# Unmasked even-head queries, score matmuls over 16 rows, more reciprocals broadcast by DMA, and a reordered head and tail in a two-layer attention and feed-forward kernel

## The chip, the cores and the metric

The kernel runs on one NeuronCore of a Trainium2 chip. The core has TensorE (PE: matrix products), VectorE (DVE), ScalarE (ACT: the exponentials here), GpSimd (POOL) and SyncE (SP: it issues DMA transfers). The metric is device time in microseconds (us); a smaller number is better. A half per cent of it is about 8 us.

## The reference

The input x has 2048 rows of 512 numbers. Two layers are applied to it one after the other, and both use the same weights. Cut to what matters:

```python
def _A_ref(x, wqkv, wo):                       # 32 heads of 16 columns each
    q, k, v = split((x @ wqkv))
    scores = einsum("bhqd,bhkd->bhqk", q, k) * 16 ** -0.5
    return merge(einsum("bhqk,bhkd->bhqd", softmax(scores), v)) @ wo

def _B_ref(x, w1, w2):                         # 512 -> 1792 -> 512
    return maximum(x @ w1, 0) @ w2

for layer in range(2):
    x = x + _A_ref(_layernorm(x), wqkv, wo)
    x = x + _B_ref(_layernorm(x), w1, w2)
```

A layer's softmax has 32 x 2048 x 2048 scores, so 134 million exponentials. In units of 128 x 512 scores that is 2048 blocks a layer, 4096 in all.

## The kernel before, in words

**Layout.** Scores are kept transposed: 128 keys lie on the partitions, and 512 queries (256 in the last chunks of layer 1) on the columns. A tile of Q or K holds eight heads, four pairs of them; each pair lies on 32 partitions, 16 for the even head (e = 0) and 16 for the odd one (e = 1). A score matmul multiplies all 32 partitions of a pair, with Q masked so that only the wanted head counts: `q_masked` (L637) reads the Q projection out of PSUM once and writes it twice, multiplied by two columns of `qmask` that hold the softmax scale for one head and zero for the other. Four such matmuls, one for each pair, run in four strips of 32 rows of TensorE.

**Slots.** The main loop (`while units`) works in slots of three blocks of 512 score columns, in one of two PSUM tiles `ps_s`. ScalarE takes the exponential of the whole slot (L1323, 1536 columns), or of two blocks of it (1024 columns); then VectorE takes the third block, with an approximation of its own: a line (`lin`, L1008, integer arithmetic that yields the bits of a float), and, once two such halves make a pair, a `chain` of bit operations and products (`step`, `cube`, L1049 to L1064). The products of exponentials and V (L914) add up in one PSUM bank, `ps_o`, for each segment, which is one head (of each of four pairs) for one chunk of queries and some of the keys. V carries columns of ones, so the same matmuls give the softmax sums.

**The end of a segment** (`finish_segment`). VectorE copies `ps_o` to a tile `u` (L836), or adds stored partial sums to it (L834) when the segment is the second part of a head ("load"). SyncE gathers the row of sums to a small tile `c`, VectorE takes the reciprocals (L860), SyncE writes them back, and they are spread over the head's rows into `r`: by a DMA that GpSimd issues (L863), or, where the segment is "quick", by a shuffle on VectorE (L873). A product (L849) writes the attention output `ot`. A segment is quick if it has partial sums to load or is the last of its chunk. The last two segments take the reciprocals after the spread, without the small transfers (`direct`).

**The other work**, the projections, layer norms, output projection and feed-forward of each chunk, is cut into groups of matmuls (L442) with an evacuation by VectorE, and is fitted between the slots. The order is written when the program is built: a planner keeps clocks for TensorE, VectorE and ScalarE (`now_pe`, `now_dve`, `exp_end`) with costs and lags (`R_LAG` = 10500 ns until a broadcast by DMA is there, `C_LAG` = 3600 ns) and picks what comes next. `rank` orders VectorE's tasks: chains rank below other tasks, but above them when the current segment has at most `HASTE` blocks left. A score matmul is repeated where the planner sees TensorE idle (`times`), to keep it busy. At run time each engine executes its list in order and waits on semaphores.

**Layer norm.** `ln_stats` (L477, L478) takes statistics of a tile of 128 rows, `ln_rstd` and `ln_newton` the reciprocal root (a seed from bits and Newton steps; the steps on GpSimd in the main loop, on VectorE in the head and the tail), `ln_apply` (L519) the normalisation.

**Head and tail.** In the head the first four tiles of x are normalised, transposed and projected to K, Q and V for the first slots; dummy matmuls (L1082) run meanwhile. In the tail, after the last exponential, the last 256 rows go through the output projection, layer norm and feed-forward. The 14 column blocks of w1 come through four rotating buffers `w1buf`; `load_w1` (L675) issues the next load when a buffer has been used, in the tail as well.

## Time and profile before

| what | value |
|---|---|
| median of 3 runs | 1608.02 us (1604.52 to 1611.87) |
| profiled execution, its own time | 1608.03 us |
| profiled execution, span of its instructions | 1606.2 us |
| mean granted TensorE clock | 0.992 |
| ScalarE busy | 1558.0 us (97%) |
| VectorE busy | 1505.7 us (94%) |
| TensorE busy (matmul) | 1446.1 us (90%) |
| first exponential starts | 16.74 us |
| last exponential ends | about 1576.7 us |

The profile gives for each group of instructions its source line, engine, operation, what it writes and reads, and the count; after the bar the busy time, the mean duration of one in ns, and the idle time of the engine just before them, with the instructions that ended it. Instructions of one engine can overlap by a little, so the mean duration is somewhat more than the busy time divided by the count. In a view by stretches each engine has its busy time in the stretch; then come the granted clock of TensorE as a share of full speed, the share of time of the DMA engines, and GB/s.

### The profile page before, as it was taken

The numbers are of one execution on the slowest core, as the hardware profiler recorded it, in microseconds if no ns is written. First come the engines' busy times: TensorE is split into PE (matmuls) and PEld (weight loads), VectorE is DVE, ScalarE is ACT, GpSimd is POOL, SyncE is SP. The second block draws the span as 40 slices with busy tenths as digits, with TensorE's granted clock in tenths as the row PEclk, the third lists the DMA queues.
The fourth block names the chain that finished last, engine by engine and source line by source line (L and its number), as shares of the span: only waits on it lengthen the run. The fifth ranks groups of instructions, "written<-read, shape, count | busy, mean of one in ns | idle before, by whom it ended". The sixth has DMA issues, their size and how long they took to land. (4 is left out here: it accounts for less than half of the span.)

```text
span 1606.2 us, 45384 instructions
## 1 busy us (share of the span) xinstructions
PE 1446.1 (90%) x19833; PEld 541.9 (34%) x19833; DVE 1505.7 (94%) x3012; ACT 1558.0 (97%) x1385; POOL 92.9 (6%) x279
## 2 busy tenths in 40 slices
PE   7988888999999988999889998889989999998997
PEld 3322222322332332232223333223334444544454
DVE  7779999999999999999899999899999999999994
ACT  6999999999999999999999999999999999999994
POOL 2000001000010010100100000001001010010100
PEclk9999999999999999999999999999999999999999
DMA  5000000210001100120001000000210211212031
GB/s 164 2 2 2 2 2 9 47 29 10 9 17 40 28 16 2 27 50 10 15 2 27 21 2 1 2 4 9 54 24 17 42 30 29 59 28 54 14 62 47
DMA packets 113928, 40.61 MB, mean 25 GB/s; under 512 B 103328, under 2 KB 111264, under 8 KB 113728
## 3 DMA queue, kind: packets, MB, share of 16 engines
q1 hardware_dynamic: 101696, 26.21, 7.2%
q0 software_dynamic: 10688, 10.18, 3.6%
q8 instruction: 155, 2.54, 0.7%
q10 hardware_dynamic: 1344, 1.31, 0.2%
q14 instruction: 45, 0.37, 0.1%
HBM read 24.38 MB, written 2.10 MB: 16 GB/s over the span
## 5 line engine op out<-in xcount | busy, mean ns | idle before, releaser
L1323 ACT ACTIVATE e<-ps_s 128x1536 bf16<-128x1536 f32 (+1 forms) x1366 | 1548.1, 1364 | 12.4 <-PE ps_s L1314 7.7
L1314 PE MATMUL ps_s<-q,ktp 32*128 32x512 bf16 (+1 forms) x6192 | 613.6, 341 | 112.2 <-ACT e L1323 97.5
L914 PE MATMUL ps_o<-e,vaug 128*32 128x512 bf16 (+1 forms) x4262 | 501.0, 346 | 16.6 <-DVE u L836 6.8
L1008 DVE TENSOR_SCALAR lin<-ps_s 128x512 int16<-128x512 f32 x680 | 462.3, 684 | 32.9 <-PE ps_s L1314 27.4
L1314 PEld LDWEIGHTS <-ktp 32*128 32x128 bf16 x6192 | 199.9, 91 | 561.5 <-issue 417.5
L914 PEld LDWEIGHTS <-vaug 128*32 128x32 bf16 x6032 | 171.5, 94 | 305.0 <-issue 286.2
L1049 DVE TENSOR_SCALAR step<-lin 128x1024 int16<-128x1024 int16 x680 | 266.2, 417 | 1.1 <-PE ps_o L914 0.4
L1060 DVE TENSOR_TENSOR cube<-step 128x1024 f16<-128x1024 bf16 x340 | 230.2, 680 | 0.9
L1064 DVE TENSOR_TENSOR cube<-cube,lin 128x1024 bf16<-128x1024 f16 x340 | 229.5, 677 | 0.0
L914 PE MATMUL ps_o<-step,vaug 128*32 128x512 bf16 (+1 forms) x858 | 154.3, 341 | 0.0
L442 PE MATMUL ps_f<-xnT,w 128*32 128x512 bf16 (+1 forms) x2016 | 147.4, 345 | 5.7 <-DVE ht L695 3.7
L442 PE MATMUL ps_f<-w,ht 128*32 128x512 bf16 x1624 | 147.1, 381 | 1.6 <-DVE q L637 0.6
L914 PE MATMUL ps_o<-cube,vthird 128*32 128x512 bf16 (+1 forms) x804 | 140.0, 339 | 0.0
L914 PE MATMUL ps_o<-lin,vaug 128*32 128x512 bf16 (+1 forms) x858 | 118.9, 341 | 4.6 <-DVE u L836 3.7
L442 PE MATMUL ps_f<-xnT,wqkv 128*32 128x512 bf16 (+1 forms) x1312 | 106.7, 363 | 3.6 <-DVE vaug L623 1.8
L863 POOL DMA_DIRECT2D r<-u x52 | 36.9, 710 | 1170.2 <-DVE step L1049 383.3
L442 PE MATMUL ps_f<-wo,ot 128*32 128x512 bf16 x960 | 87.1, 381 | 1.5 <-DVE x L661 0.7
L695 DVE TENSOR_SCALAR ht<-ps_f 128x512 bf16<-128x512 f32 x105 | 71.8, 684 | 3.6 <-PE ps_f L442 3.0
L442 PEld LDWEIGHTS <-w 128*32 128x32 bf16 x2016 | 58.4, 96 | 36.0 <-issue 19.2
L637 DVE TENSOR_TENSOR q<-ps_f,masks 128x1024 bf16<-128x1024 f32 (+1 forms) x51 | 53.5, 1049 | 3.5 <-PE ps_s L1314 2.6
L442 PEld LDWEIGHTS <-ht 128*32 128x32 bf16 x1624 | 47.0, 96 | 27.3 <-issue 12.1
L849 DVE SCALAR_TENSOR_TENSOR ot<-u,masks,r 128x512 bf16<-128x512 f32 (+2 forms) x82 | 51.0, 624 | 1.1
(86 smaller groups left out, 653.4 us busy)
## 6 DMA issues: line engine op xcount, KB each, us to landing
w<-in_B_w_dram SPq DMA_DIRECT2D x140, 128.0 KB
r<-u POOLq DMA_DIRECT2D x25, 256.0 KB, 7.3
r<-u POOLq DMA_DIRECT2D x27, 128.0 KB, 4.9
out_dram<-x SPq DMA_DIRECT2D x16, 128.0 KB
x<-in_A_x_dram SPq DMA_DIRECT2D x14, 128.0 KB
w<-in_B_w_dram SPq DMA_DIRECT2D x1, 1792.0 KB
wqkv<-in_A_wqkv_dram ACTq DMA_DIRECT2D x2, 512.0 KB
c<-u SPq DMA_DIRECT2D x48, 8.0 KB
```

The costliest lines, as they stand in the source:

```text
L442: nc.tensor.matmul(out[cols], lhsT[:, cols], rhs, start=i % k == 0, stop=i % k == k - 1, tile_position=(0, 32 * g), skip_group_check=True,)
L637: return nc.vector.tensor_mul(out=qbuf[n % 2][:, :, 0:w], in0=b.rearrange("p (e q) -> p e q", e=1).to_broadcast((P, 2, w)), in1=qmask.rear ...
L695: nc.vector.tensor_scalar(out=out, in0=sums, scalar1=0.0, scalar2=None, op0=ALU.max)
L849: nc.vector.scalar_tensor_tensor(out=ot[t][:, at_column + a : at_column + a + w], in0=u[:, a : a + w], scalar=mask[e], in1=r[:, a : a + w] ...
L863: nc.gpsimd.dma_start(out=r[:, 0:width], in_=bass.AP(tensor=sums.tensor, offset=sums.offset, ap=[list(sums.ap[0]), [0, 32], [1, width]],),)
L914: nc.tensor.matmul(ps_o[32 * g : 32 * g + 32, 0 : sg["w"]], values[:, 4 * sg["T"] + g, 2 * e : 2 * e + 32], rhs, start=g not in sg["begun" ...
L1008: first = nc.vector.tensor_scalar(out=lin[which][:, half * QS : (half + 1) * QS], in0=src, scalar1=EXP_BIAS, scalar2=0.0, op0=ALU.add, op1 ...
L1049: nc.vector.tensor_scalar(out=stair, in0=line, scalar1=keep, scalar2=put, op0=ALU.bitwise_and, op1=ALU.bitwise_or,)
L1060: (609, lambda: nc.vector.tensor_mul(out=power, in0=mantissa, in1=mantissa)),
L1064: (609, lambda: nc.vector.tensor_mul(out=power.bitcast(BF16), in0=power, in1=line.bitcast(BF16))),
L1314: nc.tensor.matmul(b[:, a : a + sg["w"]], kt[32 * g : 32 * g + 32, kc : kc + P], qbuf[sg["n"] % 2][32 * g : 32 * g + 32, sg["e"], 0 : sg[" ...
L1323: ex = nc.scalar.activation(out=eb[:, 0 : place[m]], in_=b[:, 0 : place[m]], func=ACTF.Exp, scale=1.0 / (LOG2E * UNIT),)
```

## The change

- **Q and scores.** The Q projection is copied with the scale as a factor, unmasked, for the even heads (`q_raw`), and a second instruction masks that copy for the odd heads (`q_odd`). A score matmul of an even head works over the first 16 partitions of its pair, one of an odd head over all 32. `qmask` is gone.
- **Reciprocals.** A segment with partial sums to load is quick only if it is among the last three of its chunk; the others are spread by DMA. Spread and product are tasks of their own.
- **Chains.** The raised rank now holds for the chains of every segment with at most 8 blocks left, counting all blocks and not only VectorE's, instead of the current segment with at most 12.
- **V.** A slot no longer forces the V of its keys to be made; the products with V are taken only when their V is there.
- **Layer norm.** The statistics of a chunk are taken first and aggregated together (`ln_seed`); the seed takes one bit operation less; in the head and the tail the root (`ln_root`) has one third-order step and one Newton step in place of three Newton steps.
- **Head.** Only the first V tile is made ahead of the loop, its copy goes to VectorE, the copies of the transposed x change engines, and there are more dummy matmuls.
- **Tail.** The last segment's sums are read out of PSUM with no copy. w1 for the last chunk is loaded when the last but two chunk ends: four blocks in `w1buf`, ten in tiles that held K of layer 0.

```diff
-    HASTE = 12
+    HASTE = 8
...
-        return 1.5 if sg is segs[seg_at[0]] and sg["left"] <= HASTE else 3
+        return 1.5 if sg["left"] <= HASTE else 3
...
-        st = stats[i % 2]
-        nc.vector.bn_stats(out=st[:], in_=x_t[tt][:])
-        nc.vector.bn_aggr(out=mv[ln_n(tag)][:, i, :], in_=st[:])
+        nc.vector.bn_stats(out=stats[ln_n(tag)][:, i, :], in_=x_t[tt][:])
...
+    def ln_root(tag, rows):
...
+        ln_seed(tag, rows, GAIN)
+        a, y, t1 = va_[n][:, 0:rows], ya_[n][:, 0:rows], ta_[n][:, 0:rows]
+        stt = nc.vector.scalar_tensor_tensor
+        nc.vector.tensor_mul(out=t1, in0=y, in1=y)
+        nc.vector.tensor_mul(out=t1, in0=t1, in1=a)
+        stt(out=t1, in0=t1, scalar=-10.0 / 3.0, in1=t1, op0=ALU.add, op1=ALU.mult)
+        stt(out=y, in0=t1, scalar=5.0, in1=y, op0=ALU.add, op1=ALU.mult)
+        stt(out=t1, in0=y, scalar=-0.5 / GAIN, in1=y, op0=ALU.mult, op1=ALU.mult)
+        nc.vector.tensor_mul(out=t1, in0=t1, in1=a)
+        stt(out=y, in0=t1, scalar=1.5, in1=y, op0=ALU.add, op1=ALU.mult)
...
-    def q_masked(n, b, w=QS):
-        return nc.vector.tensor_mul(
-            out=qbuf[n % 2][:, :, 0:w],
-            in0=b.rearrange("p (e q) -> p e q", e=1).to_broadcast((P, 2, w)),
-            in1=qmask.rearrange("p (e q) -> p e q", q=1).to_broadcast((P, 2, w)),
+    def q_raw(n, b, w=QS):
+        return nc.vector.tensor_scalar(
+            out=qbuf[n % 2][:, 0, 0:w], in0=b, scalar1=SCALE * LOG2E * UNIT, scalar2=None,
+            op0=ALU.mult,
+        )
+
+    def q_odd(n, w=QS):
+        nc.vector.tensor_scalar(
+            out=qbuf[n % 2][:, 1, 0:w], in0=qbuf[n % 2][:, 0, 0:w], scalar1=mask[1],
+            scalar2=None, op0=ALU.mult,
         )
...
         def fin(b):
-            q_masked(n, b, w)
-            mark(("q", n))
+            q_raw(n, b, w)
+            evac.appendleft((76 + 0.26 * w, 0.0, odd))
...
-        if n < len(chunks) * NF:
+        if n < len(chunks) * NF - NF + NW1:
...
+        if (l, j) == (1, LAST - 2):
+            for ft in range(NF):
+                home = (
+                    w1buf[((l * NQS + LAST) * NF + ft) % NW1] if ft < NW1
+                    else (kt01 + kt2)[(ft - NW1) // 2][:, ft % 2, :].rearrange(
+                        "p (c f) -> p c f", c=NDC
+                    )
+                )
+                w1_last.append(home)
+                if ft >= NW1:
+                    nc.sync.dma_start(
...
-        quick = sg["load"] is not None or ended[l, j] == NT
+        quick = ended[l, j] == NT or sg["load"] is not None and ended[l, j] >= NT - 2
...
+            source = ps_o if last else u
...
-    idle_matmuls(18)
+    idle_matmuls(24)
...
-        copy = nc.scalar.copy if i % 2 else nc.vector.tensor_copy
+        copy = nc.vector.tensor_copy if i > 1 else nc.scalar.copy
...
-    for kb in range(2):
-        b = plain(v_mms(kb))
-        uses(nc.scalar.copy(out=v_out(0, kb), in_=v_in(b)), in_bank[0])
-        mark(("v", 0, kb))
-    work.extend(v_group(0, kb) for kb in range(2, TPC))
+    b = plain(v_mms(0))
+    uses(nc.vector.tensor_copy(out=v_out(0, 0), in_=v_in(b)), in_bank[0])
+    mark(("v", 0, 0))
+    work.extend(v_group(0, kb) for kb in range(1, TPC))
...
-    now_pe[0] = 12000.0
-    now_dve[0] = 13400.0
-    exp_end = {-1: 13600.0, 0: 13600.0}
+    now_pe[0] = 13160.0
+    now_dve[0] = 14500.0
+    exp_end = {-1: 12600.0, 0: 13600.0}
...
-        for sg, kb, g in taken:
+        for sg, kb, g in now:
             sg["left"] -= 1
...
+                rows = slice(32 * g, 32 * g + 16 * (1 + sg["e"]))
...
-                    kt[32 * g : 32 * g + 32, kc : kc + P],
-                    qbuf[sg["n"] % 2][32 * g : 32 * g + 32, sg["e"], 0 : sg["w"]],
+                    kt[rows, kc : kc + P],
+                    qbuf[sg["n"] % 2][rows, sg["e"], 0 : sg["w"]],
...
-        for sg, kb, g in now:
-            run_until(("v", sg["l"], kb))
```

## The prediction
> **What bounds the kernel now.** I read the page's first two parts, then the groups of instructions kept apart by shape, the waits of ScalarE, and the stretches and timelines of head, tail and worst place. The page:

> ```profile
> span 1606.2 us, 45384 instructions
> PE 1446.1 (90%) x19833; PEld 541.9 (34%) x19833; DVE 1505.7 (94%) x3012; ACT 1558.0 (97%) x1385; POOL 92.9 (6%) x279
> ACT  6999999999999999999999999999999999999994
> ```

> ScalarE is full from the second slice to the last but one. The groups by shape (busy us, mean ns of one, idle before):

> ```profile
> L1323 ACT ACTIVATE e<-ps_s 128x1536 bf16<-128x1536 f32 x685 | 1026.9, 1574 | 8.2 <-PE ps_s L1314 4.2 <-PE ps_o L914 3.6
> L1323 ACT ACTIVATE e<-ps_s 128x1024 bf16<-128x1024 f32 x680 | 733.1, 1153 | 4.2 <-PE ps_s L1314 3.5 <-PE ps_o L914 0.4
> L637 DVE TENSOR_TENSOR q<-ps_f,masks 128x1024 bf16<-128x1024 f32 x35 | 42.6, 1217 | 2.4 <-PE ps_s L1314 1.7 <-PE ps_f L442 0.4
> L873 DVE STREAM_SHUFFLE r<-u 128x512 f32<-128x512 f32 x23 | 16.7, 727 | 0.0
> ```

> So the time is a head until the first exponential, one stream of 1366 exponentials with only 12.4 us of visible idle time, and a tail. A block of 512 scores that VectorE takes over is worth 1574 - 1153 = 421 ns of ScalarE. The head and the tail, from ScalarE's timeline (start, duration):

> ```profile
> 14.79 0.59 ACT L1128 CAST vaug<-ps_f 128x512 bf16<-128x512 f32 x1 [1.14 <-PE ps_f L1116]
> 15.65 0.59 ACT L1128 CAST vaug<-ps_s 128x512 bf16<-128x512 f32 x1 [0.28 <-PE ps_s L1116]
> 16.74 1.45 ACT L1323 ACTIVATE e<-ps_s 128x1536 bf16<-128x1536 f32 x1 [0.51 <-PE ps_s L1314]
> ...
> 1566.61 10.10 ACT L1323 ACTIVATE e<-ps_s 128x1536 bf16<-128x1536 f32 x8
> 1581.14 1.07 ACT L1387 CAST x<-ps_s 128x512 bf16<-128x512 f32 x2 [4.42 <-PE ps_s L1377]
> ```

> Head 16.7, stream to 1576.7, tail 29.5 us. Where the stream's idle time lies, by stretches (length, busy of PE, PEld, DVE, ACT, POOL, then the granted clock):

> ```profile
> 152.00:154.00 2.00, 0.92 (x11) 0.35 (x14) 2.00 (x4) 1.60 (x3) 0.00 (x0) 1.00 0.00 0
> 154.00:156.00 2.00, 1.22 (x15) 0.31 (x13) 1.09 (x3) 0.86 (x1) 0.00 (x0) 0.61 0.03 8
> 158.00:160.00 2.00, 2.00 (x15) 0.24 (x9) 1.14 (x2) 1.02 (x1) 0.00 (x0) 0.50 0.00 0
> ...
> 1588.00:1590.00 2.00, 2.00 (x10) 1.05 (x8) 0.42 (x1) 0.38 (x1) 0.00 (x0) 0.51 0.19 43
> ```

> VectorE is full (2.00 of 2.00) while TensorE has nothing to do (0.92), then the clock halves and ScalarE starves for ten microseconds: in 152 to 166 it is busy 9.22 of 14, 4.8 lost. The same pattern at 268 to 276 loses 1.0 and at 390 to 402 1.2. These three dips hold 7.0 of the 12.4 us. The last row is such a dip in the tail.

> [...] the longest idle stretch ahead of the tail's dip is 1.77 us (1584.58 to 1586.35), so partial idleness suffices. [...] 16 rows instead of 32 should cost a score matmul nothing. No 16-row matmul is in this trace. [...] the split q is one slow pass of 512 and a cheap second one. The trace agrees: 684 ns for 128x512 out of PSUM, 404 for the bf16 normalisation and 293 for the 544-wide vthird.

> **The change, part by part**, against the profiled execution: span 1606.2, its own time 1608.03 us, 1.8 around it, which is the median of the runs (1608.02).

> *Head, 2.2 us.* Measured before: last stats instruction done 6.7, normalisation 9.14, first K matmul 12.00, q 13.92 to 15.15, scores 16.31, exponential 16.74. The root takes 12 small instructions from 6.76 to 9.14, 0.20 each; 9 remain: 0.6 earlier; the four aggregations after the four stats run back to back, about 0.05. Copies of xnT: ScalarE takes the first two, VectorE the last two (0.42 instead of 0.59 for the last), another 0.15. First K matmul about 11.2. The K and Q weights don't block: x loads that wait for the same semaphores are issued by SyncE at 9.54 and 9.92; the one behind V's weights at 12.74. K and q take 1.89 (eight matmuls), to 13.1; the raw copy 0.68, to 13.8; the odd half and V's copy come after it, and the even heads don't need them. V's four matmuls end about 14.0, three score matmuls follow at once, without the 12 of the next q group (0.83) that stand ahead of them now, nor ScalarE's two V casts. Exponential at about 14.4 to 14.6: 2.2 saved. If V's weights came late, 0.5 less. Six more dummy matmuls (0.21 each warm) end near 8, before the transposes.

> *Stream, 3.4 us.* The built program has 677 wide and 688 narrow exponentials where there were 685 and 680: 8 x 0.421 = 3.4. VectorE pays with four chains: two line steps (1.37), two step passes (0.83), two products (1.36), 3.56 each, +14.2. It gets back: 36 wide q at 1.22 become 0.684 + 0.40 (0.29 at the least), -4.8 (to -8.8); 16 narrow ones 0.683 become 0.42 + 0.25, nothing; 11 shuffles of 0.727 gone, -8; one small instruction of 0.17 less in 15 roots, -2.6; one V copy more in the stream and one in the head, +1.4. Net about zero: VectorE stays at 94%. The matmuls rise by 92 of 19833 (all fillers among the scores), nothing while ScalarE is busier.

> *The dips, 3 us, my least certain term.* At 150.9 to 153 VectorE ran a shuffle (0.72), a product (0.75) and, just before, a 1.23 us q; a line step came late and score matmuls waited 1.25 us for it: then the clock fell. The shuffles of such segments become DMAs and the q stays in one piece of 0.68, so this place should lose less, and the raised rank of chains that are soon needed brings their results earlier. Bounds: 7.0 if all three dips vanish, -7 if as much comes anew elsewhere. I take 3: somewhat more than half of the largest dip.

> *More broadcasts on POOL's queue, nothing.* 36 wide ones instead of 25. They land 4.6 to 7.8 us after issue; with about 2.5 from reciprocal to issue that is at most 10.3, under the 10.5 that the planner waits, and no VectorE wait on such a landing is in the list of waits. What waits behind one on POOL is a root of twelve small instructions, planned with 5 us. Uncovered, each late microsecond stops VectorE's queue, a line step with it.

> *w1 loaded ahead.* The 10 SyncE issues of 128 KB move from the tail to the end of the last but two chunk. They stand before one 4 KB column read: 10 x 0.37 to 0.95 us of issue, hidden if the segment's sums come later than that. In the tail SyncE's loads now take 1588.40 to 1597.9, and the feed-forward matmuls at 1599.00 wait: steps of 0.87 (1596.73, 1597.60) become 1.40, 0.53 saved.

> *Tail, 1.25 + 0.7.* Dropping the copy of the last sums (0.47) is worth nothing: TensorE's 17 matmuls from 1577.26 end at the same time as the last product (1580.89), and the first cast at 1581.14 waits for TensorE. The root: 3 x 0.20 plus 0.06 of stats = 0.7. The w1 wait: 0.53. The idle stretch shrinks from 1.77 to about 1.1, so the dip at 1588.4 (some 2.9 us at half clock, 1.4 lost) may go: even odds, 0.7.

> Sum: 2.2 + 3.4 + 3.0 + 1.25 + 0.7 = 10.5; 1608.0 - 10.5 = 1597.5.

> **Rivals.** *A, only the ends pay.* New dips eat what the stream gains: 2.2 + 1.25 = 3.5, 1604.5. For it: the planner's order changes everywhere, waits on TensorE are scattered (18 for scores); against: VectorE's heaviest spot is relieved. *B, all dips go:* 2.2 + 3.4 + 7.0 + 1.25 + 1.4 = 15.3, 1592.8. For it: the three have one cause; against: the two later ones have no shuffle. *C, slower: broadcasts come late.* Short segments end every 6 to 8 us between 1030 and 1075, where shuffles are now replaced; if two overlapping 256 KB broadcasts land later than the planner's 10.5 us, VectorE's queue stands, TensorE idles and the clock halves. To end above 1616 it must lose 8.1 plus the 10.5 expected, 18.6 us, 1.7 for each of 11: landings some 9.5 us after issue (10.5 - 2.5 + 1.7), where 7.8 was the longest. *D, the edit doesn't act:* 16 rows are no faster, and are not counted as faster; if they cost even 10 ns each on half of 6285 matmuls, run four abreast, 8 us of a TensorE with 10% free, about 1 on the end.

> **How the numbers follow.** The sum as worked 0.50 (own range 1592 to 1603), A 0.27, B 0.15, C 0.08 (D inside the first). Half a per cent, about what a measurement tells from no change, is below 1600.0 or above 1616. Below: 0.72 of the first, all of B, a tenth of A, 0.54. Above: C, 0.08. The range 1589 to 1611 leaves out C and the far side of B.

> **What would show it.** First exponential at 14.5, narrow ones 688, no clock of 0.5 near 150 to 166, tail of 27.5 to 28.3 from the last exponential, no wait on w1 in it. Wrong if ScalarE's idle time in the stream is over 12 us, or VectorE waits for broadcasts.

## The result, and the profile after

The changed kernel took 1667.99 us (median of 4 runs, 1661.17 to 1673.46), the kernel before 1607.34 beside it: a ratio of 1.037, 95% interval 1.032 to 1.042. It became some 60 us slower where some 10 us faster was forecast. The profiled execution has a span of 1671.5 us. Its page, the lines that answer to those shown of before, with the row of the granted clock:

```profile
span 1671.5 us, 45644 instructions
PE 1538.1 (92%) x19925; PEld 542.6 (32%) x19925; DVE 1497.3 (90%) x3043; ACT 1567.2 (94%) x1383; POOL 102.7 (6%) x290
ACT  7999889999999999999999999979899999899994
PEclk9988668999999999899988998858899999999899
```

ScalarE does the same work as before and is 94% busy instead of 97%. TensorE is busy for 92 us more, with 0.5% more matmuls: it ran slower. The last row shows where. The granted clock falls to 0.5 or 0.6 in two regions, near 160 to 250 us and near 1100 us, where the ScalarE row has two of its 8s and its 7. The groups by shape:

```profile
L1367 ACT ACTIVATE e<-ps_s 128x1536 bf16<-128x1536 f32 x677 | 1010.8, 1549 | 40.0 <-PE ps_s L1358 36.6 <-PE ps_o L948 1.6
L1367 ACT ACTIVATE e<-ps_s 128x1024 bf16<-128x1024 f32 x688 | 735.1, 1131 | 31.2 <-PE ps_s L1358 29.5
L1358 PE MATMUL ps_s<-q,ktp 16*128 16x512 bf16 x1939 | 342.6, 424 | 39.0 <-ACT e L1367 33.7 <-DVE ktp L588 1.2 <-DVE u L860 0.6
L1358 PE MATMUL ps_s<-q,ktp 32*128 32x512 bf16 x1960 | 338.8, 413 | 33.2 <-ACT e L1367 29.6 <-DVE lin L1055 0.4 <-DVE mv L482 0.2
```

The exponentials are the 677 wide and 688 narrow ones that the prediction counted, and each takes no longer than before. But ScalarE stands idle for 71.2 us before them instead of 12.4, and nearly all of that is ended by score matmuls. The last two rows are a trap. The mean duration of a 16-row score matmul (424 ns) is hardly above that of a 32-row one (413), so nothing seems to be wrong with 16 rows. A view by stretches shows that both kinds suffer in the same places (length, busy time of PE, PEld, DVE, ACT, POOL, then the granted clock):

```profile
156.00:186.00 30.00, 29.94 (x194) 5.53 (x196) 22.29 (x43) 23.65 (x20) 0.68 (x1) 0.50 0.07 12
186.00:200.00 14.00, 11.92 (x128) 3.60 (x123) 12.64 (x25) 13.49 (x14) 0.68 (x1) 0.98 0.12 21
200.00:230.00 30.00, 29.75 (x197) 5.74 (x199) 22.20 (x43) 23.30 (x21) 0.00 (x0) 0.50 0.02 2
...
280.00:360.00 80.00, 72.55 (x860) 23.84 (x856) 79.06 (x160) 80.00 (x72) 6.07 (x15) 1.00 0.18 37
```

For 30 us at a time TensorE is busy without a gap (29.94 of 30) at a clock of 0.50, and ScalarE gets work for 23.65 of the 30. Between 280 and 360, where projections and feed-forward matmuls are fitted between the scores, nothing is lost. In the first region the clock falls (at 155.9, 200.2 and 244.6 us) some microseconds after score matmuls of even heads begin to prevail, near 152, 196 and 240, and returns twice (at 186.6 and 231.0) some ten microseconds after those of odd heads have taken over, and once (at 261.7) when projections come in.

### The profile page after: what moved, and what is told of

The parts are those of the page before. It is cut to its first block, busy times and chain, and to the rows that moved or that the text cites. A ratio compares the mean times of both kernels' runs of the same rounds, so it can differ in the third digit from the quotient of the medians.

```text
span 1671.5 us, 45644 instructions
## 1 busy us (share of the span) xinstructions
PE 1538.1 (92%) x19925; PEld 542.6 (32%) x19925; DVE 1497.3 (90%) x3043; ACT 1567.2 (94%) x1383; POOL 102.7 (6%) x290
## 4 chain that ended last, share of the span: by engine, by line
ACT 60%; PE 23%; DVE 13%; issue 2%; DMA 1%; SPq 1%; ACTq 0%; DVEq 0%
ACT e L1367 60%; PE ps_s L1358 9%; PE ps_o L948 7%; PE ps_f L442 4%; DVE lin L1055 4%; DVE step L1096 2%; DVE cube L1111 2%; DVE cube L1107 2%; PE ps_s L1419 1%; DVE ht L705 1%; SPq L770 1%; DMA c<-u 1%; DVE q L638 0%; DVE ot L878 0%; DMA wqkv<-in_A_wqkv_dram 0%
## 5 line engine op out<-in xcount | busy, mean ns | idle before, releaser
L1367 ACT ACTIVATE e<-ps_s 128x1536 bf16<-128x1536 f32 (+1 forms) x1366 | 1558.5, 1338 | 71.2 <-PE ps_s L1358 66.1
L1358 PE MATMUL ps_s<-q,ktp 32*128 32x512 bf16 (+3 forms) x6245 | 660.3, 365 | 91.4 <-ACT e L1367 80.3
L948 PE MATMUL ps_o<-e,vaug 128*32 128x512 bf16 (+1 forms) x4252 | 526.7, 365 | 11.4 <-DVE u L862 4.4
L1358 PEld LDWEIGHTS <-ktp 32*128 32x128 bf16 (+1 forms) x6245 | 196.4, 93 | 583.6 <-issue 436.5
L948 PE MATMUL ps_o<-step,vaug 128*32 128x512 bf16 (+1 forms) x868 | 166.7, 362 | 3.0 <-DVE step L1096 3.0
L442 PE MATMUL ps_f<-xnT,w 128*32 128x512 bf16 (+1 forms) x2016 | 152.9, 355 | 5.0 <-DVE ht L705 3.4
L442 PE MATMUL ps_f<-w,ht 128*32 128x512 bf16 x1624 | 147.4, 381 | 2.1 <-DVE ht L705 1.3
L948 PE MATMUL ps_o<-cube,vthird 128*32 128x512 bf16 (+1 forms) x814 | 146.8, 358 | 0.2 <-DVE cube L1111 0.2
L948 PE MATMUL ps_o<-lin,vaug 128*32 128x512 bf16 (+1 forms) x868 | 129.6, 365 | 3.7 <-DVE u L862 2.4
L892 POOL DMA_DIRECT2D r<-u x63 | 45.2, 717 | 1219.3 <-DMA u<-c 378.9
L442 PE MATMUL ps_f<-xnT,wqkv 128*32 128x512 bf16 (+1 forms) x1312 | 107.6, 374 | 3.8 <-DVE vaug L624 0.9
L442 PE MATMUL ps_f<-wo,ot 128*32 128x512 bf16 x960 | 92.3, 401 | 1.0 <-DVE x L671 0.4
L442 PEld LDWEIGHTS <-w 128*32 128x32 bf16 x2016 | 60.0, 98 | 35.4 <-issue 19.9
L442 PEld LDWEIGHTS <-ht 128*32 128x32 bf16 x1624 | 45.9, 96 | 27.7 <-issue 12.5
L948 PEld LDWEIGHTS <-vthird 128*32 128x32 bf16 x814 | 41.3, 97 | 33.1 <-issue 29.5
L878 DVE SCALAR_TENSOR_TENSOR ot<-u,masks,r 128x512 bf16<-128x512 f32 (+1 forms) x78 | 49.4, 633 | 0.3 <-DMA r<-u 0.3
```

The costliest lines, as they stand in the source:

```text
L442: nc.tensor.matmul(out[cols], lhsT[:, cols], rhs, start=i % k == 0, stop=i % k == k - 1, tile_position=(0, 32 * g), skip_group_check=True,)
L878: nc.vector.scalar_tensor_tensor(out=ot[t][:, at_column + a : at_column + a + w], in0=u[:, a : a + w], scalar=mask[e], in1=r[:, a : a + w] ...
L892: nc.gpsimd.dma_start(out=r[:, 0:width], in_=bass.AP(tensor=sums.tensor, offset=sums.offset, ap=[list(sums.ap[0]), [0, 32], [1, width]],),)
L948: nc.tensor.matmul(ps_o[32 * g : 32 * g + 32, 0 : sg["w"]], values[:, 4 * sg["T"] + g, 2 * e : 2 * e + 32], rhs, start=g not in sg["begun" ...
L1358: nc.tensor.matmul(b[:, a : a + sg["w"]], kt[rows, kc : kc + P], qbuf[sg["n"] % 2][rows, sg["e"], 0 : sg["w"]], start=True, stop=True, til ...
L1367: ex = nc.scalar.activation(out=eb[:, 0 : place[m]], in_=b[:, 0 : place[m]], func=ACTF.Exp, scale=1.0 / (LOG2E * UNIT),)
```

## The experiments

**Two theories.** R: 16 active rows count as less activity for TensorE's clock, so the clock halves. P: the planner's new order leaves TensorE idle, so the clock halves as it did in the three dips of before. Four kernels tell them apart. The line numbers differ by a few between them. Each ratio is to the kernel before as it ran beside that experiment (median 1608.95 us for these four, of which the one with masked Q stands further down, 1605.77 us for the later ones), and a clock is the mean of an execution.

**The change with 32 rows.** All of the change, but the even heads' score matmuls over 32 rows again. Q stays unmasked there, so the even heads' scores mix both heads of a pair: the masking is left out.

```diff
-                rows = slice(32 * g, 32 * g + 16 * (1 + sg["e"]))
+                rows = slice(32 * g, 32 * g + 32)
```

> The changed kernel with one edit: the score matmuls of the even heads work over 32 rows again, with the unmasked Q. The even heads' scores then hold both heads of a pair, so this kernel leaves the masking of the even heads out; order, instructions and durations are otherwise those of the changed kernel. Theory R (16 active rows count as less activity for TensorE's clock, so it halves in stretches that have little else to do): the mean clock goes back to 0.985 or more and the time to about 1600 us (1594 to 1608), what the rest of the change is worth. Rival P (the planner's new order, with V taken late, other chain ranks and more broadcasts, leaves TensorE idle and so lets the clock fall): the clock stays at 0.92 to 0.94 and the time at 1660 to 1673 us.

1604.39 us, ratio to before 0.997 (0.9958 to 0.9983), clock 0.986 to 0.996 instead of 0.924 to 0.935. The instructions and their order are those of the changed kernel, and 63.6 us are gone. The same two stretches:

```profile
156.00:186.00 30.00, 25.11 (x274) 7.48 (x271) 29.03 (x57) 30.00 (x28) 1.35 (x2) 1.00 0.11 18
200.00:230.00 30.00, 25.32 (x282) 7.67 (x283) 29.49 (x60) 30.00 (x29) 0.00 (x0) 1.00 0.02 2
```

TensorE has more gaps here (25.11 of 30 busy) than in the changed kernel, and keeps its full clock. P falls as the cause of this loss.

**The kernel before with 16 rows.** Q stays masked, and only the rows of the even heads' scores change.

```diff
+                rows = slice(32 * g, 32 * g + 16 * (1 + sg["e"]))
...
-                    kt[32 * g : 32 * g + 32, kc : kc + P],
-                    qbuf[sg["n"] % 2][32 * g : 32 * g + 32, sg["e"], 0 : sg["w"]],
+                    kt[rows, kc : kc + P],
+                    qbuf[sg["n"] % 2][rows, sg["e"], 0 : sg["w"]],
```

> The kernel before with one edit: the score matmuls of the even heads work over the first 16 rows of their pair; Q stays masked, so the values are the same. Theory R: the clock falls to 0.92 to 0.94, and the time rises to 1650 to 1680 us, with the half-clock stretches where even heads run without feed-forward work. Rival P: 1607 us within half a per cent, clock 0.99.

1660.23 us, ratio 1.033 (1.028 to 1.038), clock 0.934 to 0.948, so a little above the forecast in part. This edit alone makes 51.3 us of the loss (1608.95 to 1660.23), and its interval overlaps that of the whole change. The 16 rows that it takes away held zeros in Q, so rows that only multiplied zeros counted too. Its exponentials as one group, in an execution of 1649.86 us:

```profile
L1324 ACT ACTIVATE e<-ps_s 128x1536 bf16<-128x1536 f32 (+1 forms) x1366 | 1556.8, 1343 | 44.3 <-PE ps_s L1315 37.0 <-PE ps_o L914 4.9
```

**The change with 32 rows in the repeats.** Where the planner repeats score matmuls to keep TensorE busy, all but the last pass go over 32 rows. Only the last pass's scores are read.

```diff
-        for _ in range(times):
+        for rep in range(times):
...
-                rows = slice(32 * g, 32 * g + 16 * (1 + sg["e"]))
+                rows = slice(32 * g, 32 * g + (16 * (1 + sg["e"]) if rep == times - 1 else 32))
```

> The changed kernel with one edit: where a score matmul is repeated to keep TensorE busy, the repeats before the last one work over 32 rows for the even heads too; the last one, which writes what is used, over 16. Theory R: part of the activity comes back, so the clock lies between 0.94 and 0.985 and the time between 1610 and 1655 us. Rival P: no change from the changed kernel, 1660 to 1673 us.

1635.48 us, ratio 1.016 (1.010 to 1.022), clock 0.951 to 0.973. It gives back about half of the loss (1667.99 with 16 rows in the repeats, 1604.39 with 32 everywhere): more rows in matmuls whose results are thrown away made this kernel faster.

**The kernel before with 24 rows** for the even heads (the slice above with 24 in place of 16).

> The kernel before, with the score matmuls of the even heads over 24 rows instead of 32 (16 gave 1660.2 us, 32 gave 1608.9, its own time). Theory R: the fewer active rows, the oftener the clock falls: between the two, about 1615 to 1640, clock 0.96 to 0.985. If it is not the number of rows but the form (any matmul that doesn't fill its row group is handled otherwise), 24 rows cost what 16 do, about 1660.

1626.31 us, ratio 1.012 (1.009 to 1.015), clock 0.969 to 0.978. So 32, 24 and 16 rows make 1606 to 1609, 1626 and 1660 us. Here the loss grows with the number of rows taken away. If it came from a strip not being filled, 24 rows would have cost what 16 do.

**TensorE alone, by rows.** The disputed cost by itself: matmuls of 512 columns with nothing to wait for.

```diff
+    for n in range(840):
+        g = n % 3
+        nc.tensor.matmul(banks[g][:], kt[rows_of(g, 16), :], q[rows_of(g, 16), :], start=True, stop=True, tile_position=(32 * g, 0))
+    rest()      # 110 matmuls of 128 rows
```

> Leaves the whole computation out: x is copied to the output, and beside that TensorE alone runs eleven stretches of bf16 matmuls of 128 columns by 512, with no engine to wait for, each after some 24 us of whole 128-row ones: 3 row groups at once with 32, 24, 16 and 8 rows each, then 4x16, 2x32, 1x64, 1x32, 1x16, 4x8 and 4x32 rows. Theory R (the clock follows the rows that are active): 3x32 keeps 1.00, 3x16 (48 rows) falls to 0.50 within some us and stays there although TensorE is never idle, 3x8 and 1x32 too, 4x16 and 2x32 and 1x64 (64 rows) go alike; between 48 and 96 rows there is a limit. If only the time that TensorE is occupied counts, all eleven keep 1.00, and the dips of the changed kernel come from gaps between its instructions.

One execution. The stretches, in the order 3x32, 3x24, 3x16, 4x16, 2x32, 1x32 rows (busy time of PE, PEld, DVE and POOL, then the clock; ScalarE does nothing here):

```profile
36.00:95.00 59.00, 59.00 (x825) 27.14 (x819) 0.00 (x0) 0.00 (x0) 1.00 0.01 2
119.00:179.00 60.00, 60.00 (x835) 27.68 (x837) 0.00 (x0) 0.00 (x0) 1.00 0.01 2
...
211.00:319.00 108.00, 108.00 (x765) 40.62 (x762) 0.00 (x0) 0.00 (x0) 0.50 0.00 1
...
485.00:545.00 60.00, 60.00 (x1113) 28.81 (x1116) 0.00 (x0) 0.00 (x0) 1.00 0.01 2
570.00:630.00 60.00, 60.00 (x558) 26.84 (x554) 0.00 (x0) 0.00 (x0) 1.00 0.00 1
...
742.00:853.00 111.00, 111.00 (x263) 37.02 (x262) 0.00 (x0) 0.00 (x0) 0.50 0.00 0
```

TensorE is busy in every microsecond of all of them. With 48 rows at work (3x16) and with 32 the clock is 0.50; with 64 (4x16 or 2x32 alike), 72 and 96 it is 1.00. Of the stretches not shown, 1x64 and 4x32 rows keep 1.00; 3x8, 1x16 and 4x8 rows fall to 0.50. The stretches that kept the clock took 60.6 us for 280 passes, 216 ns a pass, whatever their rows. So among these stretches the row count made no difference to the duration of a matmul at full clock, but it decided the clock. The clock fell 3.3 us after the 48-row passes of the 3x16 stretch began, and 2.6 to 6.1 us after the start of the other four that fell; after the 3x16 stretch it came back some 3 us into the whole matmuls.

**TensorE alone, by columns and on the mean.** Does the clock follow rows, or cells (rows times columns)? And is it the mean that counts?

```diff
+    for n in range(280): low(52)                               # 52 rows x 128 columns; also 56, 48
+    for n in range(280): strip(0, 32)                          # 128 rows x 32 columns
+    for n in range(280): whole() if n % 2 else low(16)         # 128 rows and 16 rows in turn
```

> Leaves the whole computation out as the first measurement of TensorE alone did, with other stretches: one matmul at a time of 56, 52 and 48 rows by 128 columns (43.8, 40.6 and 37.5% of the 128 x 128 cells); 128 rows by 32 columns in one, two and three strips at once (25, 50, 75%); 128 rows by 64 columns (50%); and, in turn, whole matmuls and 16-row ones, 1 to 1 (56% on the mean), 1 to 2 (42%) and 1 to 3 (34%). If the clock follows the share of cells at work on the mean over some us, with a limit between 37.5% (3x16 rows fell) and 50% (4x16 held): 48 rows, one strip and 1 to 3 fall to 0.50; two and three strips, 64 columns and 1 to 1 hold 1.00; 56 and 52 rows and 1 to 2 narrow the limit down. If it follows rows alone, all three strips and the 64 columns hold 1.00, one strip too.

One execution. The stretches: 52 rows, 48 rows, one strip of 128 rows by 32 columns, and whole and 16-row matmuls in turn; then three matmuls of the alternation while its clock was still full (start, duration):

```profile
120.00:180.00 60.00, 60.00 (x279) 26.13 (x278) 0.00 (x0) 0.00 (x0) 1.00 0.00 1
...
208.00:319.00 111.00, 111.00 (x263) 37.24 (x262) 0.00 (x0) 0.00 (x0) 0.50 0.00 0
346.00:406.00 60.00, 60.00 (x279) 26.96 (x279) 0.00 (x0) 0.00 (x0) 1.00 0.00 1
...
690.00:829.00 139.00, 139.00 (x260) 25.90 (x259) 0.00 (x0) 0.00 (x0) 0.50 0.00 0
```

```profile
684.43 0.39 PE L65 MATMUL b<-q,kt 128*128 128x512 bf16 x1
684.75 0.39 PE L55 MATMUL b<-q,kt 16*128 16x512 bf16 x1
685.07 0.39 PE L65 MATMUL b<-q,kt 128*128 128x512 bf16 x1
```

The share of cells is refuted: a strip of 32 columns with 128 rows, a quarter of the 128 x 128 of a whole matmul, keeps 1.00, while 48 rows by 128 columns, 37.5% of it, fall. Rows count, and in these two runs the clock changes sides between 48 rows (0.50) and 52 (1.00). Of the stretches not shown, 56 rows, two and three strips and 64 columns keep 1.00; one whole matmul to two or three of 16 rows falls to 0.50. The alternation 1 to 1 was expected to hold, with 56% of the cells; it fell. Its rows agree with that: at full clock a pair of matmuls took 0.64 us (684.43 to 685.07), 0.10 us more at each change of form than a pass of one form. (128 + 16) x 0.216 / 0.64 is 48.6 rows on the mean.

**The same count in the kernel.** With each matmul's rows taken for 0.216 us per 512 columns, and strips of columns that run together counted once, the mean number of rows at work, from the trace, is:

| kernel, stretch (us) | mean rows at work | clock |
|---|---|---|
| changed, 152 to 156, 196 to 200, 240 to 244 | 41.4, 45.9, 44.2 | about 1.00, falls at the end or just after |
| changed, 160 to 176, 202 to 224, 246 to 256 | 36.4, 39.7, 37.6 | 0.50 |
| changed, 180 to 184, 224 to 228, 256 to 260 | 52.5, 51.8, 53.7 | 0.50, returns just after |
| changed, 280 to 360 | 73.3 | 1.00 |
| 32 rows, 156 to 186, 200 to 230 | 67.9, 69.2 | 1.00 |
| before, 150 to 154, 266 to 270, 1584 to 1588 | 43.3, 47.4, 48.4 | 1.00, falls at the end or just after |
| before, 200 to 230 | 67.6 | 1.00 |

As an estimate from these figures, one limit near 50 rows on the mean of some 4 us covers the two measurements of TensorE alone, the long stretches of the changed kernel and three of the dips of the kernel before. The fourth, at 393 us, it does not: 388 to 392 has a mean of 60.5 rows. Nor does every 4 us under 50 rows end in a fall.

The clock records of two of the traces suggest where to begin the count. In the kernel before, from the fall at 154.4 us on, the changes of the clock are 10.24, 105.81, 3.41, 119.47 and 6.83 us apart. Within that trace (9 changes) and within that of the changed kernel (35), all changes lie whole multiples of 3.413 us apart, to 0.002 us. So the rows are counted over the 3.413 us that end 0.2 us before each point at which a change could lie by this spacing, each matmul at its start (this gives 0 to 3 rows less than the table). The four falls of the kernel before within its first 1590 us follow 44.6, 46.6, 46.6 and 40.5 rows, and no other of these counts at full clock between 25 and 1600 us is under 48.6. A limit of 48 is then on the right side for all 454 counts at full clock in the kernel before and for 388 of 390 in the changed one, its 16 falls among them. This is an estimate from traces in which some matmuls can be missing, with the limit and the 0.2 us chosen to fit; what sets the spacing the traces don't show.

By the same estimate a dip in the changed kernel lasts for tens of microseconds because it slows the rows down. At half clock a pass takes 0.42 us instead of 0.216 (263 passes in the 111 us of the 1x32 stretch), so a TensorE that is never idle does about half as many row-passes in a microsecond. A mix of 48-row score passes and whole products then stays at 36 to 40 rows (the table's second line) until odd heads, with 96 rows a pass, come along. No experiment of its own tests this, and the returns fit it less well than the falls: 10 of 79 counts at half clock in the two traces are on the wrong side of 48.

**The rest of the change, with masked Q.** The changed kernel with the masked Q of before and 32 rows:

```diff
-                rows = slice(32 * g, 32 * g + 16 * (1 + sg["e"]))
+                rows = slice(32 * g, 32 * g + 32)
...
-            q_raw(n, b, w)
-            evac.appendleft((76 + 0.26 * w, 0.0, odd))
+            q_masked(n, b, w)
+            mark(("q", n))
```

> The changed kernel with Q masked for both heads in one pass out of PSUM as before (1.22 us instead of 0.68 and 0.3 to 0.4) and 32 rows for all score matmuls; everything else of the change stays. It is right in all values. Theory R: 1598 to 1606 us, clock 0.985 or more, a little slower than the variant with 32 rows and unmasked Q. Rival P: 1655 us or more.

1602.99 us, ratio 0.997 (0.9955 to 0.9984). The split of Q is worth nothing that these runs can tell: 1604.39 with it, 1602.99 without, where a little slower was expected. With other costs for Q the planner also built another order (683 wide exponentials instead of 677), so the two variants differ in more than Q.

**The loads of w1.** In the variant with 32 rows VectorE loses 3.0 us at 1391, waiting for a column of sums. SyncE's queue there, then VectorE's timeline (start, duration):

```profile
1381.00 8.12 SPq L770 DMA_DIRECT2D ktp<-in_B_w_dram  x10
1389.53 0.57 SPq L867 DMA_DIRECT2D c<-u  x1
```

```profile
1383.50 0.41 DVE L862 COPY u<-ps_o 128x256 f32<-128x256 f32 x1
...
1391.52 0.20 DVE L889 RECIPROCAL c<-c 128x8 f32<-128x8 f32 x1 [3.01 <-DMA c<-u]
```

The sums were copied by 1383.91. The column read could be issued only at 1389.53, behind ten loads of w1 that take 8.12 us to issue. So the loads are put two at a time behind the column reads of the next five segments:

```diff
             if sg not in segs[-2:]:
                 nc.sync.dma_start(out=c, in_=sums)
                 mark(("c", n), lag=C_LAG)
+            for ft, home in w1_later[:2]:
+                nc.sync.dma_start(out=home, in_=B_w1[:, ft * P : (ft + 1) * P].rearrange("(c p) f -> p c f", p=P))
+            del w1_later[:2]
```

> The changed kernel with masked Q and 32 rows for all heads (1603.0 us), whose ten loads of w1 are issued two behind each of the next five copies of sums instead of at once. If the burst in SyncE's queue held a reciprocal up (a wait of 2.1 us there, of 3.0 in the variant with unmasked Q), that wait goes, and 2 us with it: 1601. If the wait only hides another one, 1603.

1598.89 us, ratio 0.9948 (0.9932 to 0.9964). 2 us were forecast to go, with a wait of 2.1 us; the median is 4.1 us lower. VectorE no longer waits for a column of sums anywhere in its list of waits. The stream, from the start of the first exponential to the end of the last, is 1556.4 us (14.57 to 1570.95) where it was 1561.1 with the loads at once (15.11 to 1576.17). The stretch that held the stall:

```profile
1386.00:1397.00 11.00, 10.39 (x227) 5.44 (x229) 10.64 (x24) 11.00 (x11) 0.00 (x0) 1.00 0.45 99
```

ScalarE is full. The intervals of the two ratios to before (up to 0.9964 here, from 0.9955 there) overlap slightly, so the exact gain is open. The trace shows the wait gone, but its mean clock is also higher, 0.996 where the execution with the loads at once had 0.992, so not all of the difference need be due to the loads.

**The shuffles back as well.** The same, and every segment with sums to load is spread by VectorE again.

```diff
-        quick = ended[l, j] == NT or sg["load"] is not None and ended[l, j] >= NT - 2
+        quick = ended[l, j] == NT or sg["load"] is not None
```

> The same as the one with the loads of w1 spread, and also with the reciprocals of all segments that load earlier sums spread by a shuffle on VectorE, as in the kernel before, instead of by DMA. If late broadcasts cost more than the shuffles (one waits 2.9 us at about 1060), 1598 to 1600; if VectorE has no time to spare there, the shuffles, some 0.74 us each by the cost that the planner gives them, make it 1602 to 1606.

1599.06 us, ratio 0.9952 (0.9937 to 0.9967): no difference. VectorE waits once for a broadcast in the variant with the w1 loads spread, 2.9 us near 1060; without the 11 extra broadcasts that wait is gone, and the time stays. These last two versions are the fastest of the case, half a per cent ahead of the kernel before.

## Why the prediction was wrong, point by point

**The step that failed** is "16 rows instead of 32 should cost a score matmul nothing", with rival D, which priced 16 rows by their duration alone. It was my assumption: the trace of before has no 16-row matmul. For the duration the later runs bear it out: 216 ns a pass at full clock with 64, 72 and 96 rows at work. I carried it over to the clock, and so put the 16 rows at nothing. What came was ScalarE standing idle for 71.2 us before its exponentials, where more than 12 was named as a sign of being wrong. The prediction looked for the dips in TensorE's idle time. The measurement decides: 100% busy with 48 rows is 0.50, and 100% busy with 52 is 1.00. My own reading of the tail's dip, "partial idleness suffices", had the right sign and stopped short of asking what is counted. In hindsight the trace of before held a clue in its stretches with few projections, such as 200 to 230 at 67.6 mean rows, of which 32.5 were scores. A segment of even heads over half the rows would take 16 of them away, which leaves some 51 as an estimate: next to the 52 that kept the clock and the 48 that did not, even before anything is late.

**The dips, -3 us.** This term of the sum, with bounds of 7 each way, took no account of the rows. The 16 rows alone are worth 63.6 us (1667.99 against 1604.39). That the shuffles and the wide q cause the dips isn't shown. The three dips of before are missing in the variant with 32 rows (1.00 in 150 to 170, 268 to 276 and 390 to 402 us), but its trace has others in the stream (0.80 in 1048 to 1053, 0.72 in 1390 to 1396), and its clock over 20 executions, 0.986 to 0.996, is that of the kernel before over 32, 0.987 to 0.996. The clock differs from one execution to the next, and the time with it: in that variant executions with 0.996 took 1598.6 and 1598.9 us, those with 0.986 and 0.987 took 1607.7 to 1608.3.

**Without the 16 rows** the rest of the change is 1604.39, which is rival A's 1604.5 and not my sum of 1597.5. Rival A's reason is seen too, new dips for old ones in the stream, but that the figures meet so closely is luck: A had 2.2 of the head and 1.25 of the tail, the traces have 2.3 and 2.9, less 1.6 of the stream. The exponentials of that variant:

```profile
L1367 ACT ACTIVATE e<-ps_s 128x1536 bf16<-128x1536 f32 x677 | 1017.9, 1567 | 15.6 <-PE ps_s L1358 13.4 <-PE ps_o L948 1.6
L1367 ACT ACTIVATE e<-ps_s 128x1024 bf16<-128x1024 f32 x688 | 741.8, 1150 | 2.6 <-PE ps_s L1358 2.4
```

By the terms of the sum, in that variant:

- *Head, 2.2 us:* right. The first exponential starts at 14.44, where 14.4 to 14.6 was forecast and 16.74 measured before.
- *Stream, 3.4 us:* the count of 8 narrower exponentials was right, the gain was not realised. The stream took 1561.6 us, and 1560.0 before. ScalarE's idle time before exponentials is 18.2 us instead of 12.4. New stalls came at two places where VectorE waits for a column of sums: 2.8 us at 1049 and 3.0 at 1391, with the clock of 0.80 and 0.72 there. The first stays open: its read was issued at 1042.32 with no burst of loads ahead of it.
- *Split q:* its durations were right. The raw copy took 684 ns, the odd half 350 ns, between the 290 and 400 forecast. For 256 queries they took 415 and 284, so another 256 cost 269 ns out of PSUM and 66 within SBUF.
- *w1 loaded ahead, hidden:* wrong. The condition was put in the text ("hidden if the segment's sums come later than that"), and the sums came 5.2 us too early (1383.91, the loads' issue to 1389.12). The 0.53 us in the tail were saved: its feed-forward steps follow each other without a wait.
- *More broadcasts, nothing:* right as far as the last experiment tells: with the extra broadcasts 1598.89 us, with shuffles 1599.06. Rival C falls with it. One landing came late, but the time is no shorter without it.
- *Tail, 1.25 + 0.7:* 26.6 us from the last exponential's end where it was 29.5, so 2.9 saved and the dip of before gone. Larger than forecast; which part gave the surplus wasn't tried.

## What to carry to other kernels

Before cutting the rows of a matmul because its duration stays the same, count the mean number of rows at work over some 4 us in the stage with the least other work, and hold it against what was measured here: at 48 rows TensorE lost half its clock although it never idled, at 52 it kept it. A dummy pass, or a masked operand over full strips, can be worth having although it multiplies zeros: the full rows in the repeats gave back 32.5 us here (1667.99 to 1635.48), and taking away rows of zeros cost 51.3. And when a burst of loads is moved to another place in a queue, look at what small transfer is issued behind it and who waits for that: ten issues were 8 us.
